# Ranking six experts by their token counts on the chip, and giving each rank its own width

## The chip, the core and the metric

The kernel runs on one core of a Trainium2 chip. Its time is the device time of one execution in microseconds (us). The profile is one execution taken by the hardware profiler; its engines are PE (TensorE, matrix products), PEld (TensorE's weight loads), DVE (VectorE), ACT (ScalarE), POOL (GpSimd) and SP (SyncE, which here only issues transfers).

## The reference

A state-space layer (Mamba-2) produces 3072 token rows of 256 values. A cosine router then sends each row to the one of 8 experts whose embedding is nearest, and that expert is a two-layer network:

```python
N, D, E, F = (3072, 256, 8, 1024)
xn = x / (np.linalg.norm(x, axis=-1, keepdims=True) + 1e-06)
en = expert_emb / (np.linalg.norm(expert_emb, axis=-1, keepdims=True) + 1e-06)
logits = xn @ en.T / tau
expert_idx = np.argmax(logits, axis=1)
...
for e in range(E):
    mask = expert_idx == e
    h = np.maximum(x[mask] @ w1[e], 0.0)
    out[mask] = gate_w[mask, None] * (h @ w2[e])
```

Every value is fp32. `gate_w` is the softmax probability of the chosen expert. How many rows an expert gets is known only once the router has run. On the reference's inputs the eight experts get 408, 348, 366, 396, 382, 354, 405 and 413 rows.

## The kernel before

**The scan and the router.** The first part (`mamba`, `scan_end`) computes the layer in six chunks of 128 positions, writes the token rows to a table in DRAM (`y_rows`), and finds for each token its expert and its place in that expert's list. The list is kept in `k.idx`, a tile of 104 partitions by 8 x 4 columns: column `4*e + i` holds the tokens of expert e's i-th tile of 104 rows, plus one, and zero where there is none. `end_places` (L632) turns it into two integer tiles, `k.gi` (which row of `y_rows` to gather) and `k.to` (which row of the output to write, beyond the end where there is no token), by one subtraction and six more small DVE operations (`out_rows`, L882), and keeps the counts in `k.n`.

**Width.** Each expert has room for `CAP = 416` tokens, 4 tiles of 104. An expert with more leaves the rest to a loop of blocks of 128 (`leftover`, L1416) which is run only if there are any; a table for it is made by `leftover_blocks` (L1349), a generator of small DVE operations. `moe` advances it by three pieces at the end of each expert (L1328).

**Experts 0 and 1** are done in halves of 208 columns while the router is still finishing, by plain products (`up` L977, `down` L991). **Experts 2 to 7** take their 416 columns as two halves of m = 208 and use Strassen's scheme, seven block products in place of eight: `up_blocks` (L1056) for the first layer, `down_blocks` (L1131) for the second. The second layer of expert 7 is plain (`moe_end`). One call of `matmul` is one instruction pair in the program and, for fp32 products, two matmul records with two weight loads in the profile. So a Strassen layer is 7 products x 4 calls x 2 = 56 matmul records of 208 columns each, and an expert has 112.

**What stands on which engine.** The order is written by hand and each engine works it off in order. Around the border between two experts it is:

- PE: the seven products of `down_blocks`, with the transposes of the next expert's rows among them (`turn_x`, L961), then the next expert's `up_blocks`, with the transposes of the previous expert's outputs (`out`, L1181) between its products. In `up_blocks` four products in turn add into one PSUM bank X (a00 x00, then S1 T1, S2 T2, a11 T3), and ACT copies X out after each of the first three (`keep`, L1079: p1, u2, u3). The fourth product may only write X when the copy of u3 is done.
- DVE: the sums T of the hidden layer (L1038), the sums T1 of the next rows, the results of the products (L1148) between the sums S1 of the next first-layer weights (L1026), five small gate operations, **three pieces of `leftover_blocks`**, then the sums into the hidden layer `hT<-hp,p` (L1090), three gate operations, the four sums S of the second-layer weights (L1034), and the sums `hT<-hp,u`.
- ACT: copies p1, the relu of the sums `hT<-hp,p` (L1086, so behind them), the scaling of outputs (L1188), u2, u3.
- POOL: one gather per tile of 104 rows (L876), one scatter per tile of outputs (L1191), each an indirect transfer.
- SP: the weights of expert i + 3 are fetched at the end of expert i (`load_weights`, L79; two transfers for w1, one for w2, 2 MB in all); three buffers hold weights. The addresses are constants. Those of expert 2 are issued at L838, ahead of `first.down(1)`.

Of the kernel before, what the change touches and what calls it, by code (L numbers as in the profile page):

```python
# [8 lines left out]
F32 = mybir.dt.float32  # L9
# [8 lines left out]
Q = 128  # L18
# [7 lines left out]
CAP = TR * NT  # L26
LEFT = (T - CAP) // Q + E
HT, HALF = NT // 2, TR * NT // 2
# [50 lines left out]
def load_weights(k, e, parts=(0, 1), after=None):  # L79
    nc = k.nc  # L80
    if 0 in parts:
        k.w1t[e] = k.wp.tile([128, KD, F], F32, name="w1", tag="w1")
        for v in range(2):
            d = nc.sync.dma_start(
                k.w1t[e][64 * v : 64 * v + 64], k.w1[e].rearrange("(v z p) f -> v p z f", v=2, z=KD)[v]
            )
            if after is not None:
                hold(k, d, after)
    if 1 in parts:
        k.w2t[e] = k.wp.tile([128, KF, DM], F32, name="w2", tag="w2")  # L90
        d = nc.sync.dma_start(k.w2t[e][:], k.w2[e].rearrange("(f p) m -> p f m", p=128))
        if after is not None and 0 not in parts:
            hold(k, d, after)
# [538 lines left out]
def end_places(k):  # L632
    nc = k.nc
    n = k.pz[1][:, 456 : 456 + E]
    nc.tensor.matmul(n, lhsT=k.ones[:], rhs=k.pre[:, NU, :], start=True, stop=True)
    nc.vector.tensor_tensor(out=k.idx[:], in0=k.idx[:], in1=k.pz[0][:TR, 424 : 424 + E * NT], op=ALU.add)
    k.gi = k.const.tile([TR, E * NT], I32, name="gi")
    nc.vector.tensor_scalar(out=k.gi[:], in0=k.idx[:], scalar1=-1.0, scalar2=0.0, op0=ALU.add, op1=ALU.max)
    none = k.work.tile([TR, E * NT], F32, name="ix", tag="ix")
    nc.vector.tensor_scalar(  # L640
        out=none[:], in0=k.idx[:], scalar1=0.0, scalar2=float(T + 1), op0=ALU.is_equal, op1=ALU.mult
    )
    k.to = k.const.tile([TR, E * NT], I32, name="to")
    out_rows(k, k.mc, k.gi[:], k.to[:], none[:], "to")
    k.n = k.const.tile([128, E], F32, name="n")
    nc.vector.tensor_copy(out=k.n[:], in_=n)


# [148 lines left out]
def scan_end(k, early):  # L797
# [39 lines left out]
    late = late_jobs(k)  # L837
    load_weights(k, 2)  # L838
    first.down(1)
# [3 lines left out]
    for f in range(KF):  # L843
        second.up(f)
        if 1 <= f <= HT:
            first.out(f - 1)
    second.down(0)
    late[0].turn_x()
# [90 lines left out]
class Job:  # L939


    def __init__(s, k, nt, tr, w1, w2, p=None, bank=None):
        s.k, s.nt, s.tr, s.w1, s.w2, s.p, s.bank_ = k, nt, tr, w1, w2, p, bank
# [5 lines left out]
    def bank(s, name, bufs):  # L949
        if s.bank_ is not None:  # L950
            return s.bank_()
        return s.k.ps.tile([128, 512], F32, name=name, tag=name, bufs=bufs)

    def load(s, e):
        k = s.k
        s.x = s.tile([s.tr, s.nt, KD * Y1], "xg")
        for i in range(s.nt):
            gather(k, s.x[:, i, 0:W], k.gi[:, NT * e + i : NT * e + i + 1])
        s.to = k.to[:, NT * e : NT * e + NT]

    def turn_x(s, on_scalar=False):  # L961
        k, nc, tr, nt = s.k, s.k.nc, s.tr, s.nt
        s.xT = s.tile([128, KD, nt * tr], "xT")
        n = KD if KD * nt * tr <= 512 else 1
        for j0 in range(0, KD, n):
            t = s.bank("yp", 4)
            for j in range(j0, j0 + n):
                for i in range(nt):
                    o = ((j - j0) * nt + i) * tr
                    nc.tensor.transpose(t[:, o : o + tr], s.x[:, i, Y1 * j : Y1 * j + 128], k.ident[:tr, :tr])  # L970
            out, ps = s.xT[:, j0 : j0 + n, :].rearrange("p j m -> p (j m)"), t[:, 0 : n * nt * tr]
            if s.p is not None or on_scalar:
                s.turned = nc.scalar.copy(out=out, in_=ps)
            else:
                nc.vector.tensor_copy(out=out, in_=ps)

    def up(s, f):  # L977
        k, nc, m = s.k, s.k.nc, s.nt * s.tr
        if f == 0:
            s.hT = s.tile([128, KF, m], "hT")  # L980
        t = s.bank("hp", 3)[:, 0:m]
        for j in range(KD):
            nc.tensor.matmul(  # L983
                t, lhsT=s.w1[:, j, 128 * f : 128 * f + 128], rhs=s.xT[:, j, :], start=(j == 0), stop=(j == KD - 1)
            )
        if f % 2 == 0 or s.bank_ is not None:
            nc.scalar.activation(s.hT[:, f, :], t, ACT.Relu)
        else:
            nc.vector.tensor_scalar_max(s.hT[:, f, :], t, 0.0)

    def down(s, j, half=None, fs=range(KF)):  # L991
        k, nc, m = s.k, s.k.nc, s.nt * s.tr
        if j == 0 and not half:
            s.yT = s.tile([128, KD, m], "yoT", 2 if s.p is None else 1)
        r = slice(0, m) if half is None else slice(m // 2 * half, m // 2 * half + m // 2)
        if fs[0] == 0:
            s.yp = s.bank("yp", 4)
        t = s.yp[:, r]
        for f in fs:
            nc.tensor.matmul(  # L1000
                t, lhsT=s.w2[:, f, 128 * j : 128 * j + 128], rhs=s.hT[:, f, r], start=(f == 0), stop=(f == KF - 1)
            )
        if fs[-1] < KF - 1:
            return
        if j % 2 == 0:
            nc.scalar.copy(out=s.yT[:, j, r], in_=t)
        else:
            nc.vector.tensor_copy(out=s.yT[:, j, r], in_=t)
# [31 lines left out]
    def x_half(s, j, t):  # L1040
        m = s.nt * s.tr // 2
        return s.xT[:, j, m * t : m * t + m]

    def sum_x(s):
        s.T1 = s.tile([128, 4, s.nt * s.tr // 2], "T1", 1)
        s.sum_inputs([s.T1[:, n] for n in range(4)], [[s.x_half(j, t) for t in range(2)] for j in range(2)])

    def half(s, j, t):
        m = s.nt * s.tr // 2
        return s.hT[:, 4 * j : 4 * j + 4, m * t : m * t + m]  # L1050

    def sum_h(s):
        s.T = s.tile([128, 4, KF // 2, s.nt * s.tr // 2], "T", 1)
        s.sum_inputs([s.T[:, n] for n in range(4)], [[s.half(j, t) for t in range(2)] for j in range(2)])

    def up_blocks(s):  # L1056


        k, nc, m = s.k, s.k.nc, s.nt * s.tr // 2
        s.hT = s.tile([128, KF, 2 * m], "hT")  # L1060
        a = [[s.w1[:, j, F // 2 * i : F // 2 * i + F // 2] for j in range(2)] for i in range(2)]
# [17 lines left out]
        def keep(name, t):  # L1079
            p = s.tile([128, 2 * m], name)  # L1080
            nc.scalar.copy(out=p[:], in_=t[:, 0 : 2 * m])  # L1081
            return p
# [48 lines left out]
    def down_blocks(s):  # L1131


        k, nc, m = s.k, s.k.nc, s.nt * s.tr // 2
        s.yT = s.tile([128, KD, 2 * m], "yoT")
        w = [[s.w2[:, 4 * j : 4 * j + 4, 128 * i : 128 * i + 128] for j in range(2)] for i in range(2)]
# [13 lines left out]
        def part(name):  # L1150
            return s.tile([128, m], name, 1)[:]

# [24 lines left out]
        product(t5, s.S[:, 0], s.T[:, 0])  # L1177
        add(s.yT[:, 0, m:], t5, v)
        add(s.yT[:, 1, m:], t5, u3)

    def out(s, i, on_scalar=False):  # L1181
        k, nc, tr = s.k, s.k.nc, s.tr
        t = s.bank("ot", 1) if s.p is not None or i % 2 == 0 else s.bank("yp", 4)
        for j in range(KD):
            nc.tensor.transpose(t[:tr, 128 * j : 128 * j + 128], s.yT[:, j, tr * i : tr * i + tr], k.ident[:])
        y = s.tile([tr, DM], "yo", 4 if s.p is None else 2)
        if on_scalar:
            nc.scalar.activation(y[:], t[:tr, 0:DM], ACT.Copy, scale=s.gate[:, i : i + 1])  # L1188
        else:
            nc.vector.tensor_scalar_mul(y[:], t[:tr, 0:DM], s.gate[:, i : i + 1])  # L1190
        d = nc.gpsimd.indirect_dma_start(  # L1191
            out=k.out[:, :], out_offset=bass.IndirectOffsetOnAxis(ap=s.to[:, i : i + 1], axis=0),
            in_=y[:], in_offset=None, bounds_check=T - 1, oob_is_err=False,
        )
# [56 lines left out]
def moe(k, second, late):  # L1251

    def begin(e):
        j = Job(k, NT, TR, k.w1t[e], k.w2t[e])
        j.load(e)
        return j
# [92 lines left out]
def leftover_blocks(k):  # L1349
# [7 lines left out]
    def tt(out, in0, in1, op):  # L1357
        nc.vector.tensor_tensor(out=out, in0=in0, in1=in1, op=op)


    over = tile_("over", [128, E])
    nc.vector.tensor_scalar(
        out=over[:], in0=k.n[:], scalar1=float(CAP), scalar2=0.0, op0=ALU.subtract, op1=ALU.max
    )
    yield
# [34 lines left out]
    nf = of("left_n", over[:])  # L1400
    yield
    tt(bf[:], k.step[:], bf[:], ALU.subtract)
    nc.vector.tensor_scalar_mul(bf[:], bf[:], float(Q))
    tt(nf[:], nf[:], bf[:], ALU.subtract)
    yield
    rf = tile_("left_r", [128, LEFT])
    nc.vector.tensor_scalar(out=rf[:], in0=ef[:], scalar1=float(T), scalar2=float(CAP), op0=ALU.mult, op1=ALU.add)
    tt(rf[:], rf[:], bf[:], ALU.add)
# [183 lines left out]
```

## Time and profile before

| | us |
|---|---|
| runs | 264.57 median of 3 (264.39 to 267.73) |
| the profiled execution | 266.37, span of its instructions 264.6 |
| granted TensorE clock in it | 0.985 |
| span of experts 2 to 6, from one expert's second product of the second layer to the next's | 21.48, 21.75, 21.77, 21.48 |
| end of the last matmul | 258.65 |

A row of the profile names line, engine, operation and tiles (out <- in), and how often. The chain of waits is followed back from the last instruction: at each step to what released it. A timeline gives start, duration, engine, line and what ended the idle time before it in square brackets. A table by stage gives for each stretch of time the busy time of each engine.

### The profile page before, as it was taken

The page shows a single profiled execution, that of the slowest core. Times are in us where ns is not written, and L with a number is a line of the kernel's source. Part 1 is how long each engine was busy: PE and PEld are TensorE (multiplying, and loading weights), DVE is VectorE, ACT ScalarE, POOL GpSimd, SP SyncE. Part 2 cuts the span into 40 slices and gives each one's busy share as a digit, 9 for nine tenths or more (in the row PEclk, how much of TensorE's full clock was granted, in tenths as well). Part 3 has the DMA queues.
Part 4 walks back from the last instruction along what each step waited for, and adds up shares of the span by engine and source line. Part 5 has one row for each costly group of instructions (what it writes and reads, how often), then busy time and mean ns, then how long its engine had stood idle before and what let it go on. Part 6 is the DMA issues. An engine that isn't in the chain of part 4 may idle for free.

```text
span 264.6 us, 6644 instructions
## 1 busy us (share of the span) xinstructions
PE 247.8 (94%) x2589; PEld 230.1 (87%) x2590; DVE 173.0 (65%) x444; ACT 112.0 (42%) x308; POOL 127.9 (48%) x173
## 2 busy tenths in 40 slices
PE   6889899998899999999999999999999999999990
PEld 2678778887699999999889999989999999999980
DVE  6776888888464403153969878896896985972121
ACT  2534444242064232240474385175258357527200
POOL 8999556854412632847172075167237524005033
PEclk9999999999799999999999999999999999999996
DMA  4987764346199990698720862582292101002011
GB/s 115 303 260 212 263 204 122 113 138 140 44 284 271 231 254 29 155 262 196 216 59 22 174 203 67 128 222 78 79 264 73 50 7 52 0 0 65 5 32 32
DMA packets 22305, 35.90 MB, mean 136 GB/s; under 512 B 2547, under 2 KB 15550, under 8 KB 22272
## 3 DMA queue, kind: packets, MB, share of 16 engines
q1 hardware_dynamic: 19024, 28.73, 40.3%
q0 software_dynamic: 3072, 6.67, 9.3%
q8 instruction: 21, 0.34, 0.6%
q14 instruction: 12, 0.10, 0.1%
q10 hardware_dynamic: 176, 0.06, 0.1%
HBM read 29.05 MB, written 6.65 MB: 135 GB/s over the span
## 4 chain that ended last, share of the span: by engine, by line
PE 49%; issue 19%; POOL 18%; DVE 7%; DMA 4%; POOLq 1%; ACT 1%; DVEq 0%
PE yp L1140 15%; PE yp L1068 9%; PE hp L1068 6%; PE eb L983 4%; DMA out_dram<-yo,to 4%; PE eb L1000 4%; POOL xb L278 4%; POOL xg L876 3%; DVE g L361 3%; POOL out_dram L1191 2%; POOL xs L265 2%; POOL spread L110 1%; PE pz L613 1%; PE yp L970 1%; PE hp L983 1%
## 5 line engine op out<-in xcount | busy, mean ns | idle before, releaser
L1191 POOL DMA_INDIRECT out_dram<-yo,to x32 | 35.2, 1100 | 70.5 <-ACT yo L1188 40.4
L876 POOL DMA_INDIRECT xg<-y_rows,gi x32 | 36.7, 1148 | 15.5 <-issue 7.9
L361 DVE TENSOR_TENSOR g<-pg,mask 128x1536 f32<-128x1536 f32 x12 | 21.1, 1755 | 6.0 <-PE pg L351 6.0
L1086 ACT ACTIVATE hT<-hT 128x416 f32<-128x416 f32 x36 | 19.7, 551 | 11.4 <-DVE hT L1090 5.8
L1000 PE MATMUL yp<-hT,w 128*128 128x208 f32 x128 | 23.4, 340 | 0.3 <-PEq L1424 0.3
L1090 DVE TENSOR_TENSOR hT<-hp,u 128x416 f32<-128x416 f32 x24 | 14.0, 590 | 13.7 <-PE hp L1068 7.1
L1000 PEld LDWEIGHTS yp<-hT,w 128*128 128x128 f32 x128 | 22.3, 190 | 0.6 <-issue 0.6
L1140 PE MATMUL yp<-T,S 128*128 128x208 f32 x120 | 22.7, 339 | 0.0
L1140 PEld LDWEIGHTS yp<-T,S 128*128 128x128 f32 x120 | 21.2, 190 | 0.0
L1218 POOL TENSOR_TENSOR gr<-gr,half 104x4 f32<-104x4 f32 x8 | 8.8, 1094 | 23.8 <-ACT sq L1212 23.8
L1068 PE MATMUL yp<-T,S 128*128 128x208 f32 x96 | 19.2, 343 | 0.5 <-ACT u L1081 0.3
L1068 PEld LDWEIGHTS yp<-T,S 128*128 128x128 f32 x96 | 16.1, 190 | 1.4 <-ACT u L1081 0.8
L1140 PE MATMUL yp<-hT,w 128*128 128x208 f32 x80 | 15.7, 339 | 0.0
L1081 ACT COPY p<-yp 128x416 f32<-128x416 f32 x12 | 6.0, 498 | 22.8 <-PE yp L1068 22.7
L1140 PEld LDWEIGHTS yp<-hT,w 128*128 128x128 f32 x80 | 14.2, 190 | 0.0
L413 ACT COPY yT<-py 128x512 f32<-128x512 f32 x12 | 6.4, 589 | 15.7 <-PE py L402 15.7
L1212 ACT ACTIVATE sq<-xg 104x256 f32<-104x256 f32 x32 | 12.9, 408 | 0.0
L983 PE MATMUL eb<-xT,w 128*128 128x208 f32 x64 | 12.8, 345 | 0.0
L1081 ACT COPY u<-yp 128x416 f32<-128x416 f32 x24 | 12.0, 505 | 1.9 <-PE yp L1068 1.6
L983 PE MATMUL hp<-xT,w 128*128 128x208 f32 x64 | 12.2, 339 | 0.0
L1038 DVE TENSOR_TENSOR T<-hT 128x832 f32<-128x832 f32 x10 | 10.2, 1020 | 3.1 <-ACT hT L1086 2.5
L544 POOL TENSOR_TENSOR pre<-pre,ob 128x8 bf16<-128x8 bf16 x24 | 4.8, 199 | 15.3 <-DVE ob L539 13.8
(246 smaller groups left out, 593.3 us busy)
## 6 DMA issues: line engine op xcount, KB each, us to landing
w<-in_moe_w_dram SPq DMA_DIRECT2D x16, 512.0 KB
w<-in_moe_w_dram SPq DMA_DIRECT2D x8, 1024.0 KB
y_rows<-rows SPq DMA_DIRECT2D x6, 528.0 KB
x<-in_x_dram SPq DMA_DIRECT2D x6, 512.0 KB
ct<-in_CT_dram SPq DMA_DIRECT2D x6, 256.0 KB
bi<-in_BT_dram SPq DMA_DIRECT2D x6, 256.0 KB
b<-in_B_dram SPq DMA_DIRECT2D x6, 256.0 KB
xa<-in_x_dram SPq DMA_DIRECT2D x6, 128.0 KB
```

Source lines behind the costliest of these rows:

```text
L278: engine.tensor_tensor(out=k.xb[c % 2][p, :, :, v, :], in0=src.rearrange("p b (q d) -> p b q d", q=4), in1=r[p, :, 4 * v : 4 * v + 4].unsq ...
L361: t.masked = k.nc.vector.tensor_tensor(out=g[:], in0=k.pg[:, :, 0:384].rearrange("p q (u m) -> p q u m", u=2), in1=k.mask[:].unsqueeze(1). ...
L876: k.nc.gpsimd.indirect_dma_start(out=x, out_offset=None, in_=k.y_d[0:rows, :], in_offset=bass.IndirectOffsetOnAxis(ap=at, axis=0), bounds_ ...
L983: nc.tensor.matmul(t, lhsT=s.w1[:, j, 128 * f : 128 * f + 128], rhs=s.xT[:, j, :], start=(j == 0), stop=(j == KD - 1))
L1000: nc.tensor.matmul(t, lhsT=s.w2[:, f, 128 * j : 128 * j + 128], rhs=s.hT[:, f, r], start=(f == 0), stop=(f == KF - 1))
L1068: nc.tensor.matmul(t[:, m * u : m * u + m], lhsT=w[:, f : f + 128], rhs=x, start=start and u == 0, stop=True, skip_group_check=True,)
L1081: nc.scalar.copy(out=p[:], in_=t[:, 0 : 2 * m])
L1086: nc.scalar.activation(h, h, ACT.Relu)
L1090: nc.vector.tensor_tensor(out=h, in0=view(t), in1=view(p), op=ALU.add)
L1140: nc.tensor.matmul(t, lhsT=a[:, f], rhs=b[:, f], start=start and f == 0, stop=(f == 3), skip_group_check=True)
L1191: d = nc.gpsimd.indirect_dma_start(out=k.out[:, :], out_offset=bass.IndirectOffsetOnAxis(ap=s.to[:, i : i + 1], axis=0), in_=y[:], in_offs ...
L1212: s.k.nc.scalar.activation(sq[:], s.x[:, i, :].rearrange("p (j w) -> p j w", j=KD)[:, :, 0:128], ACT.Square, accum_out=s.r[:, i : i + 1],)
```

## The change

Experts 2 to 7 are no longer taken in the order of their numbers but by their numbers of tokens, largest first (equal numbers: lower expert first). `sort_experts` compares the six counts with each other on DVE, and makes the order (`k.order`), the rank of each expert (`k.slot`), and the list of places with its columns put in that order; `to_rows` then makes `k.gi` and `k.to` of it. `load_weights` reads the expert's number from `k.order` into a register of SP and addresses the weights by it. The i-th of the six has a width of its own, `CAPS` = 416, 408, 400, 388, 376, 364; the last tile of its four is shorter by what is missing. Products, sums and copies take that many columns (m = half of it). The room of an expert in `leftover_blocks` is computed from its rank.

```diff
+FIXED = 2
+SORTED = E - FIXED
+CAPS = [CAP - 8 * i - 4 * max(i - 2, 0) for i in range(SORTED)]
+LEFT = (T - CAPS[-1]) // Q + E
...
 def load_weights(k, e, parts=(0, 1), after=None):
+    i = slice(e, e + 1)
+    if e >= FIXED:
+        i = bass.ds(
+            nc.values_load(
+                k.order[0:1, e - FIXED : e - FIXED + 1], engines=(mybir.EngineType.SP,), min_val=0, max_val=E - 1
+            ), 1,
+        )
...
+def sort_experts(k):
+    nc.vector.scalar_tensor_tensor(
+        out=key[:], in0=k.n[:, FIXED:], scalar=float(E), in1=k.rank[:, FIXED:], op0=ALU.mult, op1=ALU.add
+    )
+    nc.vector.tensor_tensor(
+        out=p[:], in0=key[:].unsqueeze(1).to_broadcast(sq), in1=key[:].unsqueeze(2).to_broadcast(sq), op=ALU.is_ge
+    )
+    nc.vector.reduce_sum(out=k.slot[:], in_=p[:], axis=AX.X)
+    nc.vector.tensor_tensor(
+        out=p[:], in0=k.slot[:].unsqueeze(1).to_broadcast(sq), in1=k.place_at[:, 0:m].unsqueeze(2).to_broadcast(sq),
+        op=ALU.is_equal,
+    )
+    nc.vector.tensor_tensor(
+        out=e[:], in0=p[:], in1=k.rank[:, FIXED:].unsqueeze(1).to_broadcast(sq), op=ALU.mult
+    )
+    nc.vector.reduce_sum(out=key[:], in_=e[:], axis=AX.X)
+    nc.vector.tensor_scalar(
+        out=k.order[:], in0=key[:], scalar1=-1.0, scalar2=float(E), op0=ALU.mult, op1=ALU.add
+    )
+    nc.vector.tensor_tensor(
+        out=rows[:], in0=k.idx[:, FIXED * NT :].rearrange("p (e t) -> p t e", t=NT).unsqueeze(1).to_broadcast(each),
+        in1=p[:TR].unsqueeze(2).to_broadcast(each), op=ALU.mult,
+    )
+    nc.vector.reduce_sum(out=idx[:], in_=rows[:].rearrange("p s t e -> p (s t) e"), axis=AX.X)
+    to_rows(k, idx[:], FIXED * NT)
...
-    load_weights(k, 2)
     first.down(1)
...
         second.up(f)
         if 1 <= f <= HT:
             first.out(f - 1)
+        if f == HT:
+            sort_experts(k)
+            load_weights(k, FIXED)
...
-        j = Job(k, NT, TR, k.w1t[e], k.w2t[e])
+        j = Job(k, NT, TR, k.w1t[e], k.w2t[e], cols=CAPS[e - FIXED])
...
-        k, nc, m = s.k, s.k.nc, s.nt * s.tr // 2
+        k, nc, m = s.k, s.k.nc, s.cols // 2
...
-    nc.vector.tensor_scalar(
-        out=over[:], in0=k.n[:], scalar1=float(CAP), scalar2=0.0, op0=ALU.subtract, op1=ALU.max
-    )
+    nc.vector.memset(cap[:, 0:FIXED], float(CAP))
+    nc.vector.tensor_scalar(out=c, in0=k.slot[:], scalar1=-3.0, scalar2=0.0, op0=ALU.add, op1=ALU.max)
+    nc.vector.tensor_scalar(out=c, in0=c, scalar1=-4.0, scalar2=float(CAP + 8), op0=ALU.mult, op1=ALU.add)
+    nc.vector.scalar_tensor_tensor(out=c, in0=k.slot[:], scalar=-8.0, in1=c, op0=ALU.mult, op1=ALU.add)
+    yield
+    tt(over[:], k.n[:], cap[:], ALU.subtract)
+    nc.vector.tensor_scalar(out=over[:], in0=over[:], scalar1=0.0, scalar2=None, op0=ALU.max)
     yield
...
     nf = of("left_n", over[:])
     yield
+    rf = of("left_r", cap[:])
+    yield
```

In `end_places` the same seven operations that made `k.gi` and `k.to` for all 32 columns now make them for the 8 columns of experts 0 and 1. In `leftover_blocks`, `of` is one product and one reduction over LEFT x 8 values (LEFT was 28 and is 29).

## The prediction

> **What bounds the kernel now.** I read the page's busy times first, then the chain of waits, then a table by stage, then the timeline at the border between two experts.
>
> ```profile
> PE 247.8 (94%) x2589; PEld 230.1 (87%) x2590; DVE 173.0 (65%) x444; ACT 112.0 (42%) x308; POOL 127.9 (48%) x173
> ```
>
> An average over stages proves little, so the stages of experts 2 to 6 come next. Each stretch runs from one expert's second product of the second layer to the next expert's. The columns are its ends, its length, the busy time of PE, PEld, DVE, ACT and POOL, then clock, DMA share and GB/s.
>
> ```profile
> 139.42:160.90 21.48, 21.48 (x131) 21.00 (x129) 17.59 (x43) 11.72 (x32) 8.58 (x8) 1.00 0.51 131
> 160.90:182.65 21.75, 21.59 (x131) 20.98 (x129) 18.37 (x43) 11.46 (x32) 10.17 (x9) 1.00 0.51 131
> 182.65:204.42 21.77, 21.61 (x130) 20.99 (x129) 18.35 (x44) 11.36 (x32) 10.67 (x10) 1.00 0.53 136
> 204.42:225.90 21.48, 21.48 (x131) 21.00 (x129) 17.16 (x41) 11.69 (x32) 8.32 (x8) 1.00 0.12 33
> ```
>
> PE is the bound: busy throughout in two stretches and 0.16 us short in the other two. DVE is second with 17 to 18 us, DMA is half idle. From the chain of waits, one row inside expert 3 and one of the router (start, duration, what, how many):
>
> ```profile
> 74.43 0.93 PE py L421 x8
> 161.06 8.46 PE yp L1140 x48
> ```
>
> So a matmul of 208 columns comes every 8.46/48 = 176.3 ns, and one of 136 columns every 0.93/8 = 116.3 ns, both on 128x128 fp32 weights. The line through both has a slope of 60/72 = 0.833 ns per column and 3 ns fixed: time falls with columns, at least down to 136.
>
> **What narrowing takes from PE.** Half-widths fall from 208 to 208, 204, 200, 194, 188, 182. For each expert but the last 112 records lose 0, 4, 8, 14, 20 columns: 46 x 112 = 5152. The last has 56 records that lose 26 (1456), and its plain second layer has 64 records, of which the 32 of the second half shrink from 208 to 156 columns: 1664. Sum 8272 columns x 0.833 ns = 6.9 us. The last tile of each gather is turned by two transposes of as many columns as it has rows: 2 x (8+16+28+40+52) = 288 columns, 0.24 us. Output transposes stream 128 columns whatever the rows and save nothing. **-7.1 us**, all on the bound.
>
> A rule speaks against this. The Trainium skill (Perfetto Trace Analysis, "Identifying the Most-Contended Engine") calls matmul busy time a poor measure and says to judge TensorE by the busy share of LDWEIGHTS. That is 21.00 of 21.48 us here, 98%, with rows of 190 ns, and the change keeps every load. By that rule there is nothing to gain (0 us). But the rows of L421 also show 190 ns for a load while the matmuls come 116 ns apart: the row is a latency that overlaps, not a pace. The narrowest product here (156 columns, 3 + 156 x 0.833 = 133 ns) still stays above that 116. I take the rows: 7.1 us.
>
> **What the sort adds.** DVE gets 16 operations for `sort_experts`; the seven in `end_places` stay seven. 14 of them are as small as those in `end_places`, which come 0.21 us apart (86.33, 86.54), two have 144 values (128 values took 292 ns at L594, so 0.31): 14 x 0.21 + 2 x 0.31 = 3.6 us. They stand behind the second output scaling of `first`, and the next DVE work is the copy at 101.17:
>
> ```profile
> 91.58 0.48 DVE L1190 TENSOR_SCALAR yo<-eb,gate 104x256 f32<-104x256 f32 x1 [0.44 <-PE eb L983]
> 101.17 0.37 DVE L1008 COPY yoT<-eb 128x208 f32<-128x208 f32 x1 [9.11 <-PE eb L1000]
> ```
>
> A gap of 9.1 us takes 3.6: cost 0 (without that cover, 3.6). The first gather of expert 2 on POOL started at 106.2; its rows are ready at about 95.7.
>
> **The fetches.** Expert 2's three transfers move from 77.7 to 82.5 us to about 94 to 97, when the order is known; SP has nothing behind them but later fetches, the first of which waited until 107.3. A fetch of 2 MB keeps the DMA busy for some 10 us (the one issued at 188.8 ended at about 200), and DMA was idle from 100 to 104 (3 GB/s). Expert 2's weights are first used at 125.5, so about 18 us of slack remain. All six fetches gain a register load and five short instructions on SP. No row shows one; the nearest is PE's load of the leftover table and its branch, which fit into the 0.46 us between the end of its products (245.25) and 245.71. From 0 to 1 us each; I take 1, and it is hidden: a fetch is issued about 37 us ahead of the expert (188.8 for 225.9). POOL issues the same gathers and scatters as before, in the same order.
>
> **What the leftover table adds, and where it lands.** This is the cost that counts. DVE's pieces stand between the gates and `hT<-hp,p`; ACT's relu waits for that, and outputs and the copies u2, u3 stand behind it on ACT; PE's fourth product into X waits for u3. From the border of experts 3 and 4:
>
> ```profile
> 169.36 1.57 PE L1068 MATMUL yp<-xT,w 128*128 128x208 f32 x8
> 173.66 1.08 DVE L1090 TENSOR_TENSOR hT<-hp,p 128x416 f32<-128x416 f32 x2
> 177.03 0.96 ACT L1081 COPY u<-yp 128x416 f32<-128x416 f32 x2
> 177.61 1.67 PE L1068 MATMUL yp<-T,w 128*128 128x208 f32 x8 [0.17 <-issue]
> ```
>
> Let R be the start of the first product (169.36). Leftover work starts at R + 2.21 and took L = 2.09 here, so the sum starts at R + 4.30. The fourth product starts 3.95 later, at R + 8.25. At the border before, L was 0.92 and the fourth product came at R + 7.97 (147.89 to 155.86), PE's own time. So the start is R + the larger of 7.97 and 6.16 + L: 0.28 us lost here, 0.30 at the next border (L 2.11), none elsewhere: 0.58 in all.
>
> After the change DVE has seven more operations (four for the room, one more for `over`, two in the new `of`), and the pieces fall otherwise. At 0.2 us for a small one and 0.42 for one of 232 values (193.32, 193.74, 194.16), the four borders get 1.65, 1.6, 2.5 and 1.9 us. PE's own 7.97 holds five products of 8 records and shrinks by 40 x 0.833 = 33 ns per column; the chain over DVE and ACT shrinks by 9 ns (five ACT operations of two columns each at 0.8 ns, from 500 at 416 against 333 at 208, and one DVE sum). So it becomes visible earlier:
>
> - into m = 204: PE 7.84, chain 6.12 + 1.65 = 7.77: nothing.
> - into 200: 7.70 against 6.09 + 1.6 = 7.69: nothing.
> - into 194: 7.50 against 6.03 + 2.5 = 8.53: 1.0 us.
> - into 188: 7.30 against 5.98 + 1.9 = 7.88: 0.6 us.
> - into 182: no pieces left: nothing.
>
> 1.6 in place of 0.6: **+1.0 us**. The normal wait for u3 (0.06 us in every expert) grows a little, since the product beside the copy shrinks by 0.09 us and the copy by 0.04: **+0.1**. The other hand-overs have room: at 188 columns the hidden sums are ready about 1 us before their product (1.4 now), and the DVE chain to the sixth product keeps 0.1 to 0.3 us of its 0.43. I take 0 there; 0.2 us for each of five experts, 1 us, goes into the range.
>
> **Sum.** 264.6 - 7.1 + 1.0 + 0.1 = 258.6. This is against the span of 264.6, which is the median of the runs shown (264.57); the profiled execution itself took 266.37. So 258.6.
>
> **The rivals.**
> - **A, as summed**: 258.6, with its own range 257.8 to 259.3.
> - **B, no stall**: ACT's queue absorbs the leftover pieces. For it: it did at two of four borders. Against it: the two it didn't are those with L over 1.8. 264.6 - 7.1 - 0.6 = 256.9.
> - **C, DVE takes over as the bound**: it has 17 to 18 us per expert against PE's 19 to 21 after the change, it works in order, and it gains little: 38 columns of work for each column of m at 1.04 ns (370 ns at 208 against 585 at 416), so 46 x 40 ns + 0.3 = 2.1 us in all, and 1.4 in the tail, which is PE's. Less the 1.7 us of new operations this ends at 262.8; half and half with A it is 260.7. For it: the 0.43 us waits shrink. Against it: DVE sat idle 3 to 4 us in each of the stretches above.
> - **D, weight loads set the pace**: no gain, and at 208 columns the pieces cost 0.7 + 0.1 in place of 0.6: 264.8. Against it: L421.
> - **E, the fetch by register is slow, and the kernel slower than before**: place: SP's transfers. The price is 0 until a fetch takes longer than an expert, about 20 us against the 10 now; at 25 us five of them cost 25: about 285. For it: no such transfer was executed before, though the loop for leftovers holds them. Against it: the transfers, their sizes and their queue are the same; only the address differs.
> - That the change doesn't do what it says: an expert over its width would start the loop. The counts 413, 405, 396, 382, 366, 354 all stay at least 3 below; no part of my range.
>
> **How the numbers follow.** A 0.62, B 0.12, C 0.17, D 0.05, E 0.04. The prediction is A's. The range reaches to B below (256.8) and over the half-way case of C above (261.6). 2% is about what a measurement can tell from no change, a border of 259.3. Faster by more: nine tenths of A and all of B, 0.68. Within: the rest of A, C and D, 0.28. Slower: E, 0.04.
>
> **What will show it.** Matmuls of the last expert 0.155 us apart (176 now) show the slope; 176 throughout is D. Stretches of about 21.3, 20.9, 21.4 and 20.4 us in place of the four shown and a fourth product late by 1.0 and 0.6 us behind leftover rows show the stall; even stretches are B; waits of PE for DVE at L1140 are C. A DVE gap at 92 to 101 that the sort fills and an untouched 101.2 show it hidden. I am wrong above all if DVE's hand-overs inside an expert have less room than I read.

## The result, and the profile after

| | us |
|---|---|
| runs of the changed kernel | 257.82 median of 4 (257.48 to 258.42) |
| runs of the kernel before beside them | 264.91 median of 4 (264.39 to 267.73) |
| ratio | 0.971, 95% interval 0.964 to 0.979 |
| the profiled execution | 257.48, span 255.6, granted clock 0.998 |
| first product of expert 2 | 122.15 (before 125.70) |
| end of the last matmul | 250.01 (before 258.65) |

The kernel is faster by 2.9%, and 257.82 lies 0.8 us below the predicted 258.6. The views that follow show how much of that is the change. Experts 2 to 7 of the changed kernel are numbered by their place in its order, whichever expert stands there.

The busy times from the page:

```profile
PE 240.7 (94%) x2589; PEld 222.5 (87%) x2590; DVE 174.7 (68%) x467; ACT 109.8 (43%) x308; POOL 128.4 (50%) x173
```

PE has the same 2589 instructions and is 7.1 us less busy over the whole span; DVE has 23 more and still waits a third of the time. The table by stage, for the same four stretches as before (ends, length, busy time of PE, PEld, DVE, ACT, POOL, then clock, DMA share, GB/s):

```profile
135.59:156.84 21.25, 21.25 (x130) 20.79 (x129) 17.82 (x46) 11.45 (x32) 7.86 (x9) 1.00 0.52 131
156.84:177.72 20.88, 20.88 (x131) 20.44 (x129) 17.72 (x43) 11.30 (x32) 10.57 (x10) 1.00 0.56 142
177.72:199.57 21.85, 21.53 (x131) 20.10 (x129) 18.72 (x44) 11.28 (x32) 10.71 (x10) 1.00 0.52 136
199.57:220.31 20.74, 20.56 (x130) 19.66 (x129) 17.42 (x46) 10.85 (x31) 8.36 (x7) 1.00 0.14 36
```

The prediction had 21.3, 20.9, 21.4, 20.4. The first two fit. The third is 0.45 us longer than forecast and the fourth 0.3, though PE is busy nearly throughout: so PE itself does something that costs more than its columns. The chain of waits names it (start, duration, engine, tile, line, count):

```profile
177.20 0.68 PE yp L1032 x8
177.88 8.18 PE yp L1204 x48
...
198.55 1.09 PE yp L1032 x8
199.64 8.08 PE yp L1204 x48
```

L1204 is the 48 records of the second layer: 170 ns each at m = 200 (the line gives 169.6), so columns pay as forecast. L1032 is the turning of the next expert's rows, eight transposes. With a last tile of 76 rows it takes 0.68 us; with 64 rows, so with fewer columns, it takes 1.09 in this chain, and 1.18 from its start to the start of the product behind it in the timeline (198.39 to 199.57), which is the figure used from here on. No step of the prediction had this.

The border of experts 4 and 5 in the timeline (start, duration, what, and the end of the wait in brackets), against the one shown before:

```profile
185.88 1.48 PE L1132 MATMUL yp<-xT,w 128*128 128x194 f32 x8
190.55 1.02 DVE L1154 TENSOR_TENSOR hT<-hp,p 128x388 f32<-128x388 f32 x2
193.80 0.89 ACT L1145 COPY u<-yp 128x388 f32<-128x388 f32 x2
194.34 1.58 PE L1132 MATMUL yp<-T,w 128*128 128x194 f32 x8 [0.17 <-ACT u L1145]
```

R is 185.88, and the fourth product starts at R + 8.46. That is 0.96 us later than the 7.50 which the prediction reckoned as PE's own for m = 194; the late copies of u2 and u3 on ACT stand in the way. At the next border it is R + 7.65 in place of 7.30, so 0.35 late; at the other three it is on time.

The sort on DVE starts at 88.43, right behind the second output scaling, and its last operation starts at 91.78. This is what follows:

```profile
97.62 0.38 DVE L1071 COPY yoT<-eb 128x208 f32<-128x208 f32 x1 [5.66 <-PE eb L1063]
```

Of the gap of 9.11 us, 5.66 are left: the sort is hidden.

**Where the 9.0 us of the span went.** I call the time from the first product of expert 2 to the end of the last matmul the *expert part*. It is 258.65 - 125.70 = 132.95 us before and 250.01 - 122.15 = 127.86 after: -5.09. The tail behind the last matmul is 5.95 before and 5.59 after: -0.36. The other 3.55 us lie ahead of expert 2. From the first product of expert 1's first half (88.83 before, 85.28 after) to expert 2 both take 36.87 us, so these 3.55 us lie ahead of the sort, too. There, from 66 to 73 us, the trace of before has a granted clock of 0.76 and the trace after 1.00. The predicted sum for the expert part was -7.1 + 1.0 + 0.1 = -6.0. So the gain fell short by 0.9 us in the expert part, and the total still came out 0.8 lower than forecast because of the front and the tail. The experiments take both apart.

### The profile page after: what moved, and what is told of

Read it like the earlier page. It is cut to its first block, busy times and chain, and to the rows that moved or that the text cites. A ratio compares the mean times of both kernels' runs of the same rounds, so it can differ in the third digit from the quotient of the medians.

```text
span 255.6 us, 6715 instructions
## 1 busy us (share of the span) xinstructions
PE 240.7 (94%) x2589; PEld 222.5 (87%) x2590; DVE 174.7 (68%) x467; ACT 109.8 (43%) x308; POOL 128.4 (50%) x173
## 4 chain that ended last, share of the span: by engine, by line
PE 46%; POOL 19%; issue 17%; DVE 11%; DMA 5%; ACT 1%; POOLq 1%; DVEq 0%; ACTq 0%
PE yp L1204 15%; PE yp L1132 8%; PE hp L1132 5%; PE eb L1045 5%; DMA out_dram<-yo,to 5%; PE eb L1063 4%; POOL xb L289 4%; POOL xg L934 3%; DVE g L372 3%; POOL out_dram L1255 2%; POOL xs L276 2%; POOL spread L121 1%; PE yp L1032 1%; PE pz L624 1%; PE hp L1045 1%
## 5 line engine op out<-in xcount | busy, mean ns | idle before, releaser
L1150 ACT ACTIVATE hT<-hT 128x416 f32<-128x416 f32 (+5 forms) x36 | 19.0, 532 | 12.4 <-DVE hT L1154 11.4
L1063 PE MATMUL yp<-hT,w 128*128 128x208 f32 (+1 forms) x128 | 22.1, 329 | 0.5 <-ACT hT L1150 0.5
L1204 PE MATMUL yp<-T,S 128*128 128x208 f32 (+4 forms) x120 | 21.8, 331 | 0.0
L1154 DVE TENSOR_TENSOR hT<-hp,u 128x416 f32<-128x416 f32 (+5 forms) x24 | 13.3, 564 | 10.6 <-PE hp L1132 6.5
L1204 PEld LDWEIGHTS yp<-T,S 128*128 128x128 f32 x120 | 20.4, 190 | 0.0
L1132 PE MATMUL yp<-T,S 128*128 128x208 f32 (+5 forms) x96 | 18.6, 336 | 0.4 <-DVE S L1089 0.2
L1204 PE MATMUL yp<-hT,w 128*128 128x208 f32 (+4 forms) x80 | 15.1, 331 | 0.0
L1145 ACT COPY p<-yp 128x416 f32<-128x416 f32 (+5 forms) x12 | 5.7, 479 | 21.4 <-PE yp L1132 21.4
L1204 PEld LDWEIGHTS yp<-hT,w 128*128 128x128 f32 x80 | 13.7, 190 | 0.0
L1063 PE MATMUL eb<-hT,w 128*128 128x208 f32 x64 | 12.0, 341 | 0.0
L1145 ACT COPY u<-yp 128x416 f32<-128x416 f32 (+5 forms) x24 | 11.5, 485 | 1.3 <-PE yp L1132 1.1
L1101 DVE TENSOR_TENSOR T<-hT 128x832 f32<-128x832 f32 (+4 forms) x10 | 9.8, 984 | 3.0 <-ACT hT L1150 3.0
```

What stands on the lines that cost most here:

```text
L1063: nc.tensor.matmul(t, lhsT=s.w2[:, f, 128 * j : 128 * j + 128], rhs=s.hT[:, f, r], start=(f == 0), stop=(f == KF - 1))
L1132: nc.tensor.matmul(t[:, m * u : m * u + m], lhsT=w[:, f : f + 128], rhs=x, start=start and u == 0, stop=True, skip_group_check=True,)
L1145: nc.scalar.copy(out=p[:, 0 : 2 * m], in_=t[:, 0 : 2 * m])
L1150: nc.scalar.activation(h, h, ACT.Relu)
L1154: nc.vector.tensor_tensor(out=h, in0=view(t), in1=view(p), op=ALU.add)
L1204: nc.tensor.matmul(t, lhsT=a[:, f], rhs=b[:, f], start=start and f == 0, stop=(f == 3), skip_group_check=True)
```

## The experiments

The last column is the profile's; it is compared with 132.95 and 127.86.

| kernel | median us (lowest to highest) | ratio to before, 95% | expert part |
|---|---|---|---|
| before_again | 265.31 (263.90 to 267.30) | 0.999 (0.995 to 1.003) | 132.97 |
| widths_only | 260.39 (259.86 to 260.80) | 0.980 (0.975 to 0.986) | 127.89 |
| sort_416 | 265.69 (264.58 to 266.26) | 0.999 (0.996 to 1.003) | 132.71 |
| pad72 | 258.53 (257.49 to 260.30) | 0.975 (0.969 to 0.981) | 126.72 |
| early | 256.38 (256.18 to 257.18) | 0.969 (0.964 to 0.974) | 126.69 |
| early_pad | 255.17 (254.90 to 256.02) | 0.965 (0.961 to 0.969) | 125.59 |
| const_fetch | 259.61, one run | | 127.87 |
| before_early | 264.13 (262.13 to 266.51) | 0.996 (0.991 to 1.000) | 132.12 |
| adjacent | 256.66, one run | | 127.18 |
| after_again | 257.85 (257.32 to 258.60) | 0.970 (0.962 to 0.978) | 127.86 |
| widths_again | 258.52 (257.62 to 259.44) | 0.972 (0.964 to 0.981) | 127.86 |

The expert part repeats within 0.03 us for one program; what lies ahead of it doesn't. So mechanisms are judged by the expert part. A twelfth kernel, the sweep of widths, stands below.

**1. The kernel before, once more**, for what lies ahead of expert 2.

> The kernel before, unchanged, for a second profile. In the pair of profiles the first product of expert 2 starts at 125.70 us before and at 122.15 after, 3.5 us of difference ahead of any narrowed product, all of it between 66.3 and 72.6 us, where the first profile has four gaps of 0.4 us on PE with no releaser and a granted clock of 0.75. If that was an upset of one execution, this profile has none of it: first product of expert 2 near 122.2, last matmul near 255, span near 261. If the kernel before always loses it there and the change cures it, the gaps are there again and the span is near 264.6. Ratio of times 1.00 either way.

Expert 2 began at 124.63, between both numbers, with the clock at 1.00 throughout but a wait of 1.3 us for a gather (experiment 10 comes back to it). The start of expert 2 differs between executions of the same program, and a single profile can't credit it to a change.

**2. The widths alone**: order and fetches constant, fetch of expert 2 at its old place, old table of leftovers.

```diff
+ORDER = [7, 6, 3, 4, 2, 5]
...
-        i = bass.ds(
-            nc.values_load(
-                k.order[0:1, e - FIXED : e - FIXED + 1], engines=(mybir.EngineType.SP,), min_val=0, max_val=E - 1
-            ), 1,
-        )
+        i = slice(ORDER[e - FIXED], ORDER[e - FIXED] + 1)
...
+    load_weights(k, 2)
     first.down(1)
...
-            sort_experts(k)
-            load_weights(k, FIXED)
...
```

> The widths 416 to 364 without the sort: the order of the experts is a constant of the program (the order that their counts give), the weights are fetched by constant addresses at the old place, the leftover table is made as before (its room is 416 for all). My theory: the widths are the whole gain. 7.1 us of columns, less waits: the fourth product late by 0.5 and 0.6 us at the second and third border (leftover work 2.1 us each, 0.6 before), two short row transposes of 64 and 52 rows at 0.5 us each pair, 0.25 at the last layer: about 5.3 us below the kernel before. Rival: the later fetch of expert 2's weights, which leaves the DMA to the gathers, or the sort's other effects give part of it: then this kernel gains 2 to 4 us only.

The expert part is 127.89: the whole gain of the change in it, 5.1 us, comes with the widths, sort or no sort. That it agrees so closely is partly chance: the old table's pieces make the fourth product 0.44 and 0.60 us late, into m = 200 and 194, which is 0.27 us less than the new one's, and the first part of expert 2 is 0.31 us longer than in the changed kernel.

**3. Everything but the widths.**

```diff
-CAPS = [CAP - 8 * i - 4 * max(i - 2, 0) for i in range(SORTED)]
+CAPS = [CAP] * SORTED
...
-    nc.vector.tensor_scalar(out=c, in0=c, scalar1=-4.0, scalar2=float(CAP + 8), op0=ALU.mult, op1=ALU.add)
-    nc.vector.scalar_tensor_tensor(out=c, in0=k.slot[:], scalar=-8.0, in1=c, op0=ALU.mult, op1=ALU.add)
+    nc.vector.tensor_scalar(out=c, in0=c, scalar1=0.0, scalar2=float(CAP), op0=ALU.mult, op1=ALU.add)
+    nc.vector.scalar_tensor_tensor(out=c, in0=k.slot[:], scalar=0.0, in1=c, op0=ALU.mult, op1=ALU.add)
```

> The sort, the register fetches, the later fetch of expert 2 and the longer leftover table, but every width 416. My theory: nothing but the leftover pieces shows: fourth product late by 0.7 and 0.1 us in place of 0.3 and 0.3, so 0 to 0.3 us above the kernel before, and matmuls 176 ns apart throughout. Rival (the later fetch helps): 1.5 to 3.5 us below it.

The time is that of before within the spread of the runs. The expert part is 0.24 us shorter: 0.28 within expert 2, while the table's waits are 0.63 and 0.01 us in place of 0.28 and 0.30, near the 0.7 and 0.1 expected. So the sort, the order, the register fetches and the new table together cost nothing there. Expert 2 began at 125.68; but as in the first profile of before, the granted clock was 0.76 from 66 to 73 us, so this trace can't tell what the later fetch does in an undisturbed front.

**4. No transpose of a last tile under 72 rows**, to test the unforeseen rows of L1032. The rows turned in addition go to columns that nobody reads.

```diff
-                    o, p = (j - j0) * m + i * tr, s.tile_rows(i)
+                    o, p = (j - j0) * m + i * tr, max(s.tile_rows(i), 72)
```

> The changed kernel, with the transposes of each last tile made for at least 72 rows (8 or 20 rows more than are used; their columns aren't copied). In the profile after, the eight row transposes of the two narrowest experts (last tiles of 64 and 52 rows) take 1.18 us where those with 76 rows or more take 0.69. Theory: TensorE pays about 0.26 us for each transpose whose stationary operand has at most 64 rows, four of them; then this saves 1.0 us and the eight transposes take about 0.7 us again. Rival: the second half of them waits for a PSUM bank that ACT frees late; then nothing changes.

The timeline at the border of experts 5 and 6 (the row with x8 is the turning, 199.57 to 200.24):

```profile
199.57 0.83 PE L1032 MATMUL yp<-ident,xg 104*128 104x104 f32 x8
200.24 1.03 PE L1204 MATMUL yp<-hT,S 128*128 128x194 f32 x5
```

0.67 us in place of 1.18, with more rows turned, and 0.67 in place of 1.17 at the next border. The expert part is 1.14 us shorter. The median, taken on another occasion (258.53 against 257.82), doesn't show it.

**5. The two short transposes next to each other.** It tells whether a short transpose costs or the switch between short and tall.

```diff
-                for i in range(nt):
+                for i in range(nt) if j == 0 else [nt - 1, *range(nt - 1)]:
```

> The changed kernel with one order changed: in the second half of each turning the last tile goes first, so that the two short transposes of an expert stand next to each other (tall x3, short x2, tall x3), and the switch between tall and short is made twice instead of four times. Nothing else differs, and no transpose changes its size. If the switch costs (0.13 us each, from 0.53 us for four), the turnings of 64 and 52 rows take 1.18 - 0.26 = about 0.92 us. If each short transpose costs (0.26 us), they stay at 1.18. With 96, 88 and 76 rows the turning stays at 0.71 to 0.68.

```profile
198.22 1.11 PE L1032 MATMUL yp<-ident,xg 104*128 104x104 f32 x8
199.17 1.01 PE L1204 MATMUL yp<-hT,S 128*128 128x194 f32 x5
```

The turning takes 199.17 - 198.22 = 0.95 us, at the border after it too: half of the excess is gone with two of four switches, at the same sizes. The switch is what costs, 0.14 us each (1.14 us for eight of them in experiment 4, the start of the product behind the turning included). The Trainium skill (TensorEngine Tiling (Array Packing), "Key Properties") says that a change of the tiling mode drains TensorE, and under "Performance Considerations" that row tiling goes with contractions of at most 64 rows; the last tiles that cost (64 and 52 rows) and those that don't (72 and more) fall on the two sides of that. It gives no price, and the kernel asks for no tiling in these transposes. What the array does inside, no run here shows.

**6. A sweep of widths**: experts 2 to 7 at four tiles of 104, 88, 72, 64, 52 and 40 rows. Tokens beyond those are left out, so only the spacing of matmuls is read.

```diff
+ROWS = [104, 88, 72, 64, 52, 40]
...
-        j = Job(k, NT, TR, k.w1t[e], k.w2t[e], cols=CAPS[e - FIXED])
+        j = Job(k, NT, TR, k.w1t[e], k.w2t[e], rows=ROWS[e - FIXED])
...
```

> The changed kernel with experts 2 to 7 at four tiles of 104, 88, 72, 64, 52 and 40 rows each, so at half-widths of 208, 176, 144, 128, 104 and 80 columns. Tokens beyond these rows are left out, so the total time is not to be compared; what is read is how far apart the matmuls within a product come. Theory (columns alone set the pace, 3 ns and 0.833 ns a column): 176, 150, 123, 110, 90 and 70 ns. Rival (the weight load sets a floor): a floor at about 116 ns (the narrowest row seen so far) or somewhere between it and the 186-190 ns of a load; the spacing stops falling there. The turning of rows tells two forms of the short-transpose cost apart: with 64, 52 and 40 rows all eight transposes of an expert are short. If a short transpose costs 0.25 us each, the turning takes about 2 us longer; if the switch between tall and short costs (0.12 us each way), about 0.25 us longer.

From its chain of waits, at 176 and at 144 columns:

```profile
155.46 7.21 PE yp L1206 x48
...
171.83 0.98 PE yp L1206 x8
```

150.2 ns and 122.5 ns: on the line. From its timeline, at 104 and at 80 columns:

```profile
210.21 1.06 PE L1206 MATMUL yp<-T,w 128*128 128x104 f32 x8
211.10 1.06 PE L1206 MATMUL yp<-T,S 128*128 128x104 f32 x8
211.99 1.04 PE L1134 MATMUL yp<-xT,w 128*128 128x80 f32 x8
212.87 0.38 PE L1251 MATMUL ot<-ident,yoT 128*52 128x128 f32 x2
```

Groups of eight start 0.89, 0.89 and 0.88 us apart, so 111, 111 and 110 ns each, where the line has 90 and 70; at 128 columns it was 111 too. The pace stops falling at about 111 ns, or 130 columns. That is near what the Trainium skill has for a weight load (TensorE: Matmul & The Clock Gate, "LDWEIGHTS (loading the stationary operand)": 128 columns give an estimate of 107 ns), but these runs don't show the load to be the cause: transposes with a stationary operand as wide come 64 ns apart (0.51 us for eight of 72 rows). The change's narrowest product, 156 columns, stays above the floor.

The sweep's turnings agree with the switch: eight transposes of 64 rows in a row take 0.63 us where columns give 0.45, and the product behind them 0.1 us more than its columns, about 0.25 us for two switches and not 2 us for eight short transposes. With 52 and 40 rows the turning takes 0.63 and 0.62 us, so below 64 rows fewer columns save nothing here.

**7. The pieces of the leftover table moved** to the two plain experts (into their second halves), so that none stands ahead of `hT<-hp,p`.

```diff
         last, n = j, jobs[i + 1]
         n.turn_x()
+        for _ in range((7, 5)[i]):
+            next(left, None)
...
-        for _ in range(3):
-            next(left, None)
...
-        if i == E - 2:
-            for _ in left:
-                pass
```

> The changed kernel with the pieces of the leftover table moved on VectorE from the Strassen experts to the two plain experts before them (7 pieces in the first, 5 in the second, right after the turning of the next expert's rows), so that none is left between the gates and the sum hT<-hp,p. Theory (those pieces make the fourth product into X late by 0.96 and 0.36 us, through hT<-hp,p, ScalarE's relu and the copy u3): both waits become 0, and the part from the first product of expert 2 to the end of the last matmul takes 127.86 - 1.3 = 126.55 us. Rival (VectorE as a whole is what is short): the waits come back elsewhere, in the plain experts or at the start of expert 2, and first product of expert 2 begins later by as much. Rival (ScalarE's own queue): the waits stay, 127.9 us.

The border of experts 4 and 5 in its timeline:

```profile
186.88 1.48 PE L1132 MATMUL yp<-xT,w 128*128 128x194 f32 x8
189.34 1.22 DVE L1154 TENSOR_TENSOR hT<-hp,p 128x388 f32<-128x388 f32 x2 [0.18 <-PE hp L1132]
194.41 1.58 PE L1132 MATMUL yp<-T,w 128*128 128x194 f32 x8
```

DVE's sum starts at R + 2.46 in place of R + 4.67, and the fourth product at R + 7.53, without a bracket. At the next border it is R + 7.34. Both waits are gone (0.96 + 0.35 became 0.03 + 0.04), the expert part is 1.17 us shorter, and 0.1 came back in expert 2.

**8. Both**, pieces moved and no turning under 72 rows.

> The changed kernel with both edits: the pieces of the leftover table moved to the two plain experts, and no turning of a last tile with fewer than 72 rows. If the two gains are independent, the part from the first product of expert 2 to the end of the last matmul takes 127.86 - 1.3 - 1.1 = 125.4 us, and the median of the runs is about 257.8 - 2.4 = 255.4 us. If the second only uncovers another wait at the same borders (the next expert's sums T1 or S1 on VectorE), 126.0 to 126.6.

125.59 us against 125.4, and a median of 255.17 against 255.4: the gains add up. This is the version that beats both kernels, 0.965 of before (0.961 to 0.969).

**9. The pieces moved in the kernel before**, `(6, 4)` in place of `(7, 5)`.

> The kernel before with only the pieces of the leftover table moved to the two plain experts (6 and 4 pieces), all widths still 416. Theory (the prediction's R + 6.16 + L against R + 7.97): the two waits of 0.28 and 0.30 us of the fourth product go, so R to fourth product is 7.97 us at every border, and the part from the first product of expert 2 to the end of the last matmul takes 132.96 - 0.58 = 132.4 us; the median stays within 1% of before. Rival (the waits were PE's own and widen with the columns only): 133.0 us.

R to the fourth product is 7.97 or 7.98 us at all five borders, so the 0.58 us of waits in before were the table's, as read. The expert part is 0.83 us shorter: 0.58, and 0.25 within expert 2, where the change itself also gained 0.28.

**10. The sort kept, addresses of the fetches constant.**

```diff
+ORDER = [7, 6, 3, 4, 2, 5]
...
+        i = slice(ORDER[e - FIXED], ORDER[e - FIXED] + 1)
```

> The changed kernel with the sort kept, but the six weight fetches at constant addresses in the order that these tokens give (7, 6, 3, 4, 2, 5), so without register loads on SyncE. Theory (the fetch by register is hidden, cost 0): the part from the first product of expert 2 to the end of the last matmul stays at 127.9 us within 0.3; the time that SyncE takes for an issue falls from 1.41-1.47 to 1.25 us. Rival (the register fetch costs something on the path): up to 1 us less, most of it in the experts whose weights arrive last.

127.87 us. From SP's timeline, the fetch at the end of expert 4 in the changed kernel, and then in this one:

```profile
183.76 1.41 SPq L94 DMA_DIRECT2D w<-in_moe_w_dram  x2
```

```profile
185.93 1.25 SPq L91 DMA_DIRECT2D w<-in_moe_w_dram  x2
```

The register costs 0.16 us in the issue of two transfers, and nothing in the expert part.

This edit does one thing more. A constant address needn't wait for the order, so SP issues expert 2's weights 17 us earlier, ahead of the four gathers for the second halves of experts 0 and 1. The fetch on SP, PE's turning of the first gathered rows, and the time of the four gathers from issue to landing, in the changed kernel:

```profile
91.61 1.47 SPq L94 DMA_DIRECT2D w<-in_moe_w_dram  x2
94.16 0.52 PE L1032 MATMUL eb<-ident,xg 104*128 104x104 f32 x4
DMA to landing us min/median/max: 2.9/3.4/5.1
```

and in this one:

```profile
74.34 5.93 SPq L91 DMA_DIRECT2D w<-in_moe_w_dram  x2
96.36 0.49 PE L1029 MATMUL eb<-ident,xg 104*128 104x104 f32 x3 [1.80 <-DMA xg<-y_rows,gi]
DMA to landing us min/median/max: 8.2/8.4/8.7
```

With the weights on their way the gathers take 8.4 us in place of 3.4, and PE waits 1.80 us for them; this run is 1.8 us above the median of the changed kernel. The other traces agree: of the six profiles with the early fetch (two of before, two of the widths alone, experiments 9 and 10) five have a wait of 1.3 to 1.8 us at this place. The sixth, the first profile of before, came there 3.5 us later than the changed kernel and didn't wait. None of the eight with the fetch behind the sort has it. So the later fetch, which the sort forces, takes a wait off PE ahead of expert 2.

**11. The changed kernel and the widths alone, on one occasion.** Between the occasions of the first result and of experiment 2 they differed by 2.6 us, all of it outside the expert part.

> The changed kernel unchanged, once more, beside a second build of the widths alone. Its part from the first product of expert 2 to the end of the last matmul takes 127.9 us, as with the widths alone, so any difference between the two medians lies in what comes before and in the tail. If that difference (257.8 against 260.4 us so far, on two occasions) belongs to the program (the later fetch of expert 2 leaves the end of the scan undisturbed), this runs at 257.8 +- 0.6 and is 2 to 2.6 us below the widths alone. If it was the occasion, the two medians lie within 0.6 us of each other.

> The widths alone (constant order, constant addresses, fetch of expert 2 at its old place, old table) a second time, on the same occasion as the changed kernel. 260.4 +- 0.6 us if the difference to the changed kernel belongs to the program, within 0.6 us of the changed kernel if it was the occasion. Its part from the first product of expert 2 to the end of the last matmul stays at 127.9 us.

Side by side it is 257.85 against 258.52, with ranges that overlap, so most of the 2.6 us was the occasion. The 0.67 us that are left are less than the 1.3 to 1.8 us of the wait in experiment 10, and not clear of the spread of four runs each: what the later fetch is worth to the median stays open.

## Why the prediction was right, and where its sum was off

- **Columns, -7.1: right.** 48 records take 8.32 us at m = 204 and 8.18 at 200 (the line: 8.30 and 8.14), and the last expert's come 155 ns apart. The two kernels without table waits and without short turnings, experiments 9 and 8, are 132.12 - 125.59 = 6.53 us apart in the expert part, 6.8 with the 0.25 named below. That PE's busy time fell by just 7.1 on the page is chance: 1.9 of it lie ahead of expert 2, and in the expert part it fell by 5.2 (131.48 to 126.28), waits and turnings included. Of the two readings weighed, the row was right and the busy share of LDWEIGHTS (98%, no gain) was not; the section of the Trainium skill that the prediction cites for it names MFU, the share of peak operations, beside that share. The line would have failed below 130 columns.
- **Sort, 3.6 on DVE, hidden: right.** 3.5 us, and 5.66 of the gap left.
- **Fetches, hidden: right** for the register and the issue, by experiment 10. That the later fetch of expert 2 could gain something was not in the sum.
- **Leftover pieces, +1.0 (1.6 for 0.6): right in kind and nearly in size.** 0.96 and 0.35 us in place of 1.0 and 0.6: the pieces at the second of these borders took 1.72 us (the sum starts at R + 3.93, less 2.21) and not 1.9. The 0.58 of before went. So +0.7.
- **The +0.1 for the hand-over of u3** is too small to be seen on its own.
- **The term that was missing: +1.1.** "The last tile of each gather is turned by two transposes of as many columns as it has rows": for 64 and 52 rows that is the smaller part. Their eight switches between tall and short cost 1.14 us (experiments 4 and 5). The trace of before holds 104-row tiles alone at this line, so none of its rows could warn. The prediction took columns as the whole price of a transpose.
- **A second missing term: +0.25.** The last expert's plain second layer begins 0.71 us after its last first-layer product, 0.46 before. PE waits for ACT's relu now, and waited for its own sequencer then. The layer's first half is still 208 columns wide, while the Strassen half is now 182, so it needs 26 columns of sums that come last. This last step is read from the code; it was not tried. The start of the layer, after and before:

```profile
238.48 6.96 PE L1063 MATMUL yp<-hT,w 128*128 128x208 f32 x40 [0.55 <-ACT hT L1150]
```

```profile
245.71 7.27 PE L1000 MATMUL yp<-hT,w 128*128 128x208 f32 x40 [0.30 <-PEq L1424]
```

- **The first part of expert 2 became 0.28 us shorter**, where PE had waited 0.29 us for a copy of u in before. I had nothing there. In the traces, ACT's first relu of expert 2 starts 0.94 or 0.95 us after DVE's sum `hT<-hp,p` starts in before and with the widths alone, where no releaser is shown for it, and 0.61 to 0.66 us after it in the other kernels; why stays open.

Sum for the expert part: -7.1 + 0.7 + 1.1 + 0.25 - 0.3 = -5.35 against -5.09. The 0.26 us left, the +0.1 for u3 among them, are spread too thin to name.

**What lies ahead of expert 2 was not in the sum.** From median to median the time fell by 264.57 - 257.82 = 6.75 us: 5.09 in the expert part, 0.36 in the tail, and by subtraction 1.3 us ahead of expert 2 (1.6 against the 264.91 of the runs beside it). So the total was close partly because misses cancelled: 0.9 us of gain too much in the experts, 1.3 not foreseen in front of them and 0.36 behind. That was luck. For the front the record shows a cause of the right size, the wait of 1.3 to 1.8 us for a gather that goes with the later fetch (experiment 10); the prediction had moved that fetch and asked only whether it would come too late. How much of the 1.3 us it is stays open: two executions of the changed kernel began expert 2 at 122.15 and 123.27, and the medians with the fetch late and early differ by only 0.3 us (experiment 3) and 0.7 us (experiment 11).

**The rivals.** B (no stall) fell with the 0.96 and 0.35 us. C (DVE the bound) fell: in the page's group of L1204, the place that was to show it, the last column (idle time before) is zero.

```profile
L1204 PE MATMUL yp<-T,S 128*128 128x208 f32 (+4 forms) x120 | 21.8, 331 | 0.0
```

D (load pace) fell with the spacing, and the sweep shows where it would have begun. E (slow register fetch) fell with experiment 10.

## What to carry to other kernels

Read what a narrower product saves from the spacing of two shapes in the trace, and find by a sweep where that line ends. When sizes begin to vary, look up what changes in kind at a threshold, not only in amount: here a last tile of 64 rows took longer to turn than one of 76. Work that is off the bounding engine isn't free while it stands ahead of a sum that others queue behind: the same table pieces cost 1.3 us at the experts' borders and nothing in the plain stages (36.88 us from the first product of expert 1's first half to expert 2, against 36.87). And when a transfer moves, ask which other transfer it leaves alone: a term that can only cost in the sum may gain.

## What the runs showed of the hardware

- A switch between transposes of 72 or more rows and those of 64 or fewer cost PE 0.13 to 0.14 us, on average over both directions; eight short ones in a row paid for two switches only.
- fp32 matmul records on 128x128 weights came 3 ns + 0.833 ns per column apart from 208 down to 144 columns, and never closer than 110 ns at 128, 104 and 80.
- Two weight transfers addressed by a register took SP 1.41 us to issue, against 1.25 with constant addresses.
- Four gathers landed 2.9 to 5.1 us after their issue in the changed kernel, and 8.2 to 8.7 us after it where expert 2's weights (2 MB) had been issued ahead of them (experiment 10).
